# Moving two gate/up tiles out of the attention's filler, and the sums of the input ahead of its units

## The chip, the cores and the metric

The kernel runs on one core of a Trainium2 chip. The metric is the device time of one execution in microseconds. The core has TensorE (PE: matmuls, and weight loads as PEld), VectorE (DVE), ScalarE (ACT), GpSimd (POOL) and SyncE (SP, which here issues DMAs). Each works through its own instructions in order; they wait for each other by semaphores.

## The reference

Input x is 2048 × 640, 32 heads of 20, a window of 256 and a gated feed-forward of 1728.

```python
xn = _layernorm(x)
q, k, v = split_heads(xn @ wqkv)                     # wqkv 640 x 1920
scores = jnp.einsum("bhqd,bhkd->bhqk", q, k) * (Dh ** -0.5)
mask = (idx[:, None] - idx[None, :] >= 0) & (idx[:, None] - idx[None, :] < 256)
p = softmax(jnp.where(mask, scores, -1e9))
o = jnp.einsum("bhqk,bhkd->bhqd", p, v)
h = gelu(xn @ w_gate) * (xn @ w_up)                  # 640 x 1728 each
return x + o @ wo + h @ w_down
```

## The kernel before

**Arithmetic.** Activations and weights are split into a high and a low fp32r part (xh, xl; wqh, wql), and a dense product is three passes over the five blocks of 128 inputs: 15 matmuls of 128 × 512 for one tile of 128 outputs and one of the four chunks of 512 tokens.

**Stages.** First comes the layer norm chunk by chunk, with transposes into xh and xl, the first half of V (`proj_v`) and the first tiles of q and k (tile 0 and tile 5) for chunks 0 to 2. Then comes the attention: 32 units (8 groups of 4 heads × 4 chunks), each of 14 slots (NS), behind a ramp of 12 slots. Then the gate and up products of the remaining tiles, in which two chunks are joined by a scheme of seven products in place of eight (`gate_up_pair`, L953; the seven-product stage), and last the down projection (L1220).

**The attention.** A unit reads a *stack*: qs and ks, which `load_stack` (L494) loads from DRAM buffers qd and kd. `max_pair` forms scores (L523) and DVE takes their row maxima (L527); `max_end` turns these into an extra row of qs; `exp_piece` forms the scores again (L582) and ACT exponentiates them (L584) into P; `clear` has POOL zero the parts of P outside the window (L595, L598); `av_unit` multiplies with V (L609) one unit later and stores the result. Score, maximum and AV products share a ring of six PSUM banks.

**The order.** In the attention, the order on PE, ACT, DVE, POOL and SP is that in which the code emits it (`manual_schedule`). `attention()` goes from slot to slot: `at(slot, fn)` and `defer(n, fn)` put a step n slots ahead, `when_free` puts it into a list from which `release(n)` takes n steps in certain slots. Ahead of the attention a scheduler sets the order, except on PE for one chunk.

**The filler.** PE's remaining time in a slot is filled from a generator, `filler()`: projections of q and k (`proj_qk`), the second half of V (`V1_AT` says after which set) and gate/up tiles (`gate_up_fill`), in the order of the list `sets`. Each slot pulls RATE/NS matmuls, each slot of the ramp 2·RAMP. What the filler hasn't taken of the 14 gate/up tiles is left to the seven-product stage: NFA tiles and the last are in the filler.

**Saving q and k.** For each `proj_qk`, `save_qk` has ACT take the upper part (L277), DVE the remainder r (L273, one buffer), ACT the middle part (L258), POOL the lower part pt (L259), and SP store the three (L268) into qd or kd.

**The sums.** The seven-product stage reads sums of the input's two chunks that are kept in DRAM, td. `x_sums(p, k, half)` makes four of these for chunk pair p, input block k and a half chunk of 256 tokens: ten POOL instructions (L740), which POOL takes in groups of one to three for one result, and four stores (L744) on SP. Results are in tiles with two buffers. p, k and half have two values each, so there are 80 such instructions. Before, XS0 and XSN put them into units 1 to 27.

Of the kernel before, what the change touches and what calls it, by code (L numbers as in the profile page):

```python
# [9 lines left out]
F32 = mybir.dt.float32  # L10
# [20 lines left out]
NS = 14  # L31
BURSTS = 0, 4, 8
SCORES = {0: range(0, 1), 2: range(1, 5), 4: range(5, 7), 8: range(7, 9), 10: range(9, 12)}
RATE = 34.05
V1_AT = "gu", 0, 3
VEARLY = 2
VLEAD = 40
POOL_SLOTS = 13, 0, 1, 2, 3, 4, 5, 6, 7
MXD = 6
KSLOT = 9  # L40
LAG = 3, 5, 4, 4, 4, 4, 3, 3, 4, 3, 2, 1, 1, 1
NFA = 4
HD = D // 2
HR = 5
NQD = 9
OWN = 4, 5
WARM = 64
XS0, XSN = 24, 50
RAMP = 4.0
GAP = 16  # L50
VW = 1408
# [19 lines left out]
def block_kernel(ctx, tc, x, wqk, wv, wgu, wdo, wdl, out):  # L71
# [124 lines left out]
    def at(slot, fn, *a):  # L196
        acts.setdefault(slot, []).append((fn, a))
# [23 lines left out]
    def flush():  # L221
        while lates:
            fn, a = lates.pop(0)
            fn(*a)
# [4 lines left out]
    def defer(n, fn, *a):  # L229
        if now[0] is None:  # L230
            fn(*a)
        else:
            at(now[0] + n, fn, *a)

    def load_qk(t):
        raw = wrp.tile([128, KT, 128], F32, name="wr", tag="wr")
        nc.sync.dma_start(raw, wqk[t])
        return raw
# [106 lines left out]
    def first_chunk(xs, wr0, wr5, lp):  # L345
# [74 lines left out]
                save_qk(5 * i, 0, dn[i])  # L420
        return w0, w5, mv

    v0 = []
    with tc.tile_pool(name="lp", bufs=1, side="right") as lp:
        xs = [ln_load(t, lp) for t in range(2)]
        wr0 = load_qk(0)
        xs += [ln_load(t, lp) for t in range(2, 4)]
        warm = lp.tile([128, 256], BF, name="warm")[:, 0:128]
        nc.vector.memset(warm, 0.0)
        ps = psd.tile([128, C], F32, name="ps_u", tag="dn")  # L430
        for i in range(WARM):
            nc.tensor.matmul(ps[:, 0:128], warm, warm, start=True, stop=True)
        wr5 = load_qk(5)
        prep = load_v(0, v0, lp)
        next(prep)
        xs += [ln_load(t, lp) for t in range(4, 8)]
        w0, w5, mv1 = first_chunk(xs, wr0, wr5, lp)
        run(prep)
        v0 = v0[0]
        ones = lp.tile([4, 2 * C], BF, name="ones")  # L440
        nc.gpsimd.memset(ones, 0.0)
        nc.gpsimd.memset(ones[0:2], 1.0)
        for i in range(NK):
            for j in (0, 2):
                nc.sync.dma_start(ks[i][SR:64, j:j + 2].rearrange("p j t -> p (j t)"), ones)
        for c in range(1, NC):
            ln_scale(xs[4 * c:4 * c + 4], lp, mv1 if c == 1 else None)
            vs = [proj_v(v0, 4 * c - 4 + i, None if i % 2 else (psm, "mx")) for i in range(4)]
            if c == 1:
                with tc.manual_schedule(engines={mybir.EngineType.PE}):  # L450
                    lead = (cost for gen in vs for cost in gen)
                    for _ in range(VLEAD):
                        next(lead)
                    ln_turn(4 * c, xs[4 * c:4 * c + 4])
                    run(lead)
            else:
                ln_turn(4 * c, xs[4 * c:4 * c + 4])
            if c + 1 < NC:
                xs += [ln_load(t, lp) for t in range(4 * c + 4, 4 * c + 8)]
            if c == 1:  # L460
                for i in range(NQ):
                    for j in (0, 2):
                        nc.sync.dma_start(qs[i][SR + 2:64, j:j + 2].rearrange("p j t -> p (j t)"), ones[2:4])
            if c == 2:
                for z in range(4):
                    band = mask if z == 0 else lp.tile([128, D], F32, name="xi", tag="xi", bufs=8)[:, 0:288]
                    nc.gpsimd.memset(band, 0.0)
                    nc.gpsimd.affine_select(out=band, in_=band, pattern=[[1, 288]], compare_op=OP.is_ge,
                                            fill=NEG, base=32 * z - 1, channel_multiplier=-1)
                    nc.gpsimd.affine_select(out=band, in_=band, pattern=[[-1, 288]], compare_op=OP.is_ge,  # L470
                                            fill=NEG, base=256 - 32 * z, channel_multiplier=1)
                    if z:
                        nc.gpsimd.tensor_copy(mask[32 * z:32 * z + 32], band[32 * z:32 * z + 32])
                raws1 = [load_qk(1), load_qk(6)]
            if c < NC - 1:
                run(*vs)
                run(proj_qk(0, w0, c), proj_qk(5, w5, c))
            else:
                run(*[proj_v(v0, 4 * c - 4 + i) for i in range(VEARLY)])
# [204 lines left out]
                                   lambda k: xh[:, k, cs], lambda k: xl[:, k, cs], KT)  # L684
            defer(1, *((late, c4) if i else (c1,)))

    sets = [("qk", 1), ("qk", 2), ("qk", 3), ("gu", 0), ("qk", 4)]
    sets += [("gu", f) for f in range(1, NFA)] + [("gu", NF - 1)]
    pools = (wp, None), (hp, 2)
    rest = []  # L690

# [34 lines left out]
            ws = nxt  # L726
        rest.append(ws)

    def x_sums(p, k, half):
        w = C // 2  # L730
        a, b = (slice((2 * p + i) * C + half * w, (2 * p + i) * C + half * w + w) for i in (0, 1))
        eh, el = xh.bitcast(F32), xl.bitcast(F32)
        live = {}

        def tile_of(i):
            live[i] = ap.tile([128, w], F32, name="tx", tag="tx")
            return live[i]

        def pool(o, i, j, op):
            nc.gpsimd.tensor_tensor(out=o, in0=i, in1=j, op=op)  # L740

        def store(i):
            t = live[i]
            defer(4, lambda: nc.sync.dma_start(td[p][i][:, k, half * w:half * w + w], t))  # L744

        def s1():
            pool(tile_of(1), eh[:, k, b], eh[:, k, a], OP.subtract)

        def s2():
            pool(live[1], live[1], el[:, k, b], OP.add)  # L750

        def s3():
            pool(live[1], live[1], el[:, k, a], OP.subtract)
            store(1)

        def s4():
            pool(tile_of(2), eh[:, k + 2, b], live[1], OP.subtract)

        def s5():
            pool(live[2], live[2], el[:, k + 2, b], OP.add)  # L760
            store(2)

        def s6():
            pool(tile_of(4), eh[:, k + 2, a], live[2], OP.subtract)

        def s7():
            pool(live[4], live[4], el[:, k + 2, a], OP.add)
            store(4)

        def s8():  # L770
            pool(tile_of(3), eh[:, k + 2, b], eh[:, k, b], OP.subtract)

        def s9():
            pool(live[3], live[3], el[:, k + 2, b], OP.add)

        def s10():
            pool(live[3], live[3], el[:, k, b], OP.subtract)
            store(3)

        return s1, s2, s3, s4, s5, s6, s7, s8, s9, s10  # L780

    NU = NG * NC
    stream = ((u, i) for u in range(NU) for i in range(8))
    fill = filler()
# [15 lines left out]
    def pull_fill(n):  # L800
        debt[0] += n
        while debt[0] > 0:
            debt[0] -= next(fill, 1.0)

    def attention():
        now[0] = -1
        load_stack(0)
        load_stack(1)
        load_stack(2)
        for i, (p, k, half) in enumerate((p, k, half) for p in range(NC // 2) for k in range(2) for half in range(2)):  # L810
            for j, fn in enumerate(x_sums(p, k, half)):
                at(XS0 + XSN * i + 2 * j, when_free, fn)
        for i in range(12):
            now[0] = i - 13
            for fn, a in tick():
                fn(*a)
            if i % 2 == 0:
                pull_max(2, now[0])
            flush()
            pull_fill(2 * RAMP)  # L820
        pull_fill(GAP / 2)
        pull_max(2, now[0])
        pull_fill(GAP / 2)
        for u in range(NU + 1):
            for i in range(NS):
                T = now[0] = NS * u + i
                for fn, a in tick():
                    fn(*a)
                if i in BURSTS:
                    pull_max(2, T)  # L830
                if i == 0 and u:
                    av_unit(u - 1)
                    flush()
                    pull_max(2, T)
                for s in SCORES.get(i, ()) if u < NU else ():
                    exp_piece(u, s)
                flush()
                if i in POOL_SLOTS or T < NS:
                    release(2)
                if u + 3 < NU and i in (KSLOT, 12):  # L840
                    load_stack(u + 3, (int(i == KSLOT),))
                pull_fill(RATE / NS)
        while acts or idle:
            now[0] += 1
            for fn, a in tick():
                fn(*a)
            flush()
            release(2)
        assert not idle
        now[0] = None  # L850
        run(fill)
        assert not acts
# [656 lines left out]
```

## Time and profile before

| | |
|---|---|
| median of 3 runs | 1046.38 us (1045.62 to 1047.34) |
| profiled execution | 1046.71 us, span 1045.0 us |
| instructions of PE | 9533 matmul records, 99% of the span busy |
| DVE, ACT, POOL busy | 69%, 49%, 32% |
| first score matmul of the attention | at 62.42 us |
| first AV matmul (unit 0) | at 103.62 us |
| seven-product stage | from 583.30 us on, 220.37 us, 972 matmuls |

A row of a timeline has the start in us, the time it took, the engine, the line of the code, the operation, output<-inputs with their shapes, how many instructions it joins, and in brackets how long the engine stood idle ahead of it and for what. A group's row ends in busy us, mean ns | idle us ahead of it. A row of waits has the total, the number and the longest. SPq is SP's queue of DMA issues.

### The profile page before, as it was taken

To read this page: it belongs to the slowest core of one execution; us is meant where nothing else is said; L and a number is where in the kernel's file an instruction comes from. 1 tells how busy PE (TensorE), PEld (TensorE's weight loads), DVE (VectorE), ACT (ScalarE), POOL (GpSimd) and SP (SyncE) were. 2 spreads that over 40 slices of the span, in tenths; PEclk is the share of its full clock that TensorE was granted. 3 is DMA by queue.
4 is the path that set the end of the run, shared out by engine and by line. 5 is a ranking of instruction groups with operands and counts; after the bars stand their busy time and mean duration, and the time that the engine had idled before them with its cause. 6 is when DMAs were issued, how large, how long until landed. Compare 5 with 4: busy or idle time off the path is not lost.

```text
span 1045.0 us, 25814 instructions
## 1 busy us (share of the span) xinstructions
PE 1034.0 (99%) x9533; PEld 826.2 (79%) x9533; DVE 717.1 (69%) x2007; ACT 513.6 (49%) x1088; POOL 335.9 (32%) x511
## 2 busy tenths in 40 slices
PE   8999999999999999999999999999999999999998
PEld 8987666666677766666667888888888999999998
DVE  8745656666655556666663678877656888888887
ACT  4444666765665666555656522223324553333332
POOL 5222767766464458464634111110110000000000
PEclk9999999999999999999999999999999999999999
DMA  5552465545332355444322556677217864443342
GB/s 200 189 150 61 136 185 157 174 152 183 98 117 74 106 148 153 129 131 140 103 80 82 191 193 235 220 254 246 100 61 255 272 232 137 136 128 114 124 136 92
DMA packets 105192, 158.76 MB, mean 152 GB/s; under 512 B 15421, under 2 KB 60093, under 8 KB 105065
## 3 DMA queue, kind: packets, MB, share of 16 engines
q1 hardware_dynamic: 102680, 150.95, 45.1%
q10 hardware_dynamic: 2384, 6.16, 1.8%
q8 instruction: 75, 1.23, 0.5%
q14 instruction: 53, 0.43, 0.1%
HBM read 101.78 MB, written 54.92 MB: 150 GB/s over the span
## 4 chain that ended last, share of the span: by engine, by line
PE 89%; DVE 3%; DMA 3%; POOL 2%; SPq 1%; ACT 1%; issue 1%; DVEq 0%; POOLq 0%
PE ps_g L953 21%; PE ps L1220 21%; PE ps_d L110 19%; PE ps_e L582 7%; PE ps_v L110 7%; PE ps_o L609 7%; PE ps_m L523 4%; PE ps_g L110 1%; DMA qs<-qd 1%; SPq L494 1%; PE ps_t L181 1%; DMA qd<-pt 1%; POOL pt L259 1%; PE ps_d L356 1%; POOL wql L643 0%
## 5 line engine op out<-in xcount | busy, mean ns | idle before, releaser
L527 DVE CUSTOM_DVE_ANT_0 junk<-ps_m,mask 128x288 bf16<-128x288 f32 (+2 forms) x512 | 227.9, 445 | 155.0 <-PE ps_m L523 97.2
L584 ACT ACTIVATE P<-ps_e 128x512 f32<-128x512 f32 (+2 forms) x384 | 195.6, 578 | 59.8 <-PE ps_e L582 56.1
L1220 PE MATMUL ps<-wb,at 128*128 128x320 f32 x999 | 155.9, 309 | 0.0
L1220 PEld LDWEIGHTS ps<-wb,at 128*128 128x128 f32 x999 | 148.9, 188 | 0.2
L595 POOL TENSOR_SCALAR_AFFINE_SELECT P<-P 128x512 f32<-128x512 f32 x128 | 84.6, 663 | 139.1 <-ACT P L584 138.1
L582 PE MATMUL ps_e<-qs,ks 124*128 124x128 bf16 (+2 forms) x704 | 107.4, 277 | 0.6 <-DVE mx L527 0.5
L110 PE MATMUL ps_d<-xh,wqh 128*128 128x512 f32 x350 | 104.3, 410 | 0.0
L110 PE MATMUL ps_d<-xl,wqh 128*128 128x512 f32 x350 | 104.3, 409 | 0.0
L110 PE MATMUL ps_d<-xh,wql 128*128 128x512 f32 x350 | 103.9, 409 | 0.0
L1220 PE MATMUL ps<-wt,at 128*128 128x320 f32 x552 | 89.3, 309 | 0.4 <-DVE u L1058 0.4
L582 PEld LDWEIGHTS <-ks 124*128 124x128 bf16 x704 | 50.9, 98 | 46.5 <-issue 29.0
L609 PE MATMUL ps_o<-P,v 128*32 128x384 f32 (+2 forms) x1408 | 84.9, 386 | 0.7 <-POOL P L598 0.7
L1220 PEld LDWEIGHTS ps<-wt,at 128*128 128x128 f32 x552 | 82.9, 188 | 0.9 <-DVE u L1058 0.9
L598 POOL TENSOR_SCALAR_AFFINE_SELECT P<-P 128x512 f32<-128x512 f32 x112 | 70.3, 638 | 33.6 <-ACT P L584 33.6
L1174 ACT ACTIVATE at<-ss 128x512 fp32r<-128x512 f32 x59 | 37.3, 632 | 87.6 <-DVE ss L1058 87.5
L103 POOL TENSOR_TENSOR wql<-wr,wqh 128x640 fp32r<-128x640 f32 x11 | 17.6, 1607 | 174.8 <-PE ps_g L953 149.5
L609 PEld LDWEIGHTS ps_o<-P,v 128*32 128x32 f32 x1408 | 41.0, 109 | 40.5 <-issue 20.4
L110 PEld LDWEIGHTS ps_d<-xh,wql 128*128 128x128 f32 x350 | 63.9, 189 | 11.1 <-issue 0.4
L110 PEld LDWEIGHTS ps_d<-xl,wqh 128*128 128x128 f32 x350 | 63.8, 189 | 10.4 <-issue 0.2
L110 PEld LDWEIGHTS ps_d<-xh,wqh 128*128 128x128 f32 x350 | 63.5, 189 | 10.7 <-issue 0.2
L259 POOL TENSOR_TENSOR pt<-r,pt 128x512 bf16<-128x512 f32 x40 | 46.8, 1169 | 63.2 <-ACT pt L258 63.0
L613 ACT ACTIVATE ob<-ps_o 128x512 f32<-128x512 f32 x32 | 19.1, 598 | 86.3 <-PE ps_o L609 76.1
(194 smaller groups left out, 1846.8 us busy)
## 6 DMA issues: line engine op xcount, KB each, us to landing
hr<-hd SPq DMA_DIRECT2D x104, 128.0 KB
hd<-he SPq DMA_DIRECT2D x50, 256.0 KB
wr<-wgu SPq DMA_DIRECT2D x27, 320.0 KB
qs<-qd SPq DMA_DIRECT2D x64, 120.0 KB
ks<-kd SPq DMA_DIRECT2D x64, 120.0 KB
xi<-x SPq DMA_DIRECT2D x16, 320.0 KB
qs<-qd SPq DMA_DIRECT2D x64, 80.0 KB
ks<-kd SPq DMA_DIRECT2D x64, 80.0 KB
```

The lines of the kernel that those rows point to most:

```text
L110: nc.tensor.matmul(ps, a(k), b(k), start=n == 0, stop=n == 3 * nk - 1)
L259: nc.gpsimd.tensor_tensor(out=pt[:, l, :], in0=r, in1=pt[:, 1, :], op=OP.subtract)
L523: nc.tensor.matmul(ps[32 * h:32 * h + 32, lo:hi], q[rows, j, q0:q0 + 32], keys, start=True, stop=True, tile_position=(64 * r, 32 * h))
L527: nc.vector.tensor_tensor_reduce(out=junk[:, 0:n], in0=ps[:, 0:n], in1=mask[:, 288 - n:288], scale=1.0, scalar=NEG, op0=OP.add, op1=OP.max ...
L582: nc.tensor.matmul(ps[:, col:col + n], k[0:QROWS, j, kc:kc + 128], q[0:QROWS, j, q0:q0 + n], start=True, stop=True)
L584: nc.scalar.activation(pt[:, j, lo:hi], ps[:, lo:hi], AF.Exp, scale=SCALE)
L595: nc.gpsimd.affine_select(out=a, in_=a, pattern=[[0, 4], [1, 128]], compare_op=OP.is_ge, fill=0.0, base=0, channel_multiplier=-1)
L598: nc.gpsimd.affine_select(out=a, in_=a, pattern=[[0, 4], [-1, 128]], compare_op=OP.is_ge, fill=0.0, base=-1, channel_multiplier=1)
L609: nc.tensor.matmul(o[32 * j:32 * j + 32, q0:q0 + n], v[:, w0_:w0_ + 32], pt[:, j, col:col + n], start=i == 0, stop=i == len(todo) - 1, ski ...
L953: nc.tensor.matmul(ps, i, j, start=first and n == 0, stop=n == len(work) - 1, skip_group_check=True)
L1174: nc.scalar.activation(hi[:, 3:7], s, AF.Copy)
L1220: nc.tensor.matmul(ps[bank][:, 0:HD], *work[bank][j], start=bank not in begun, stop=final[p, bank] == n and j == len(work[bank]) - 1, skip ...
```

## The change

Two gate/up tiles go from the filler to the seven-product stage (NFA 4 to 2), the filler runs the four pairs of q/k tiles first and then two gate/up tiles and the last, the second half of V follows the third pair's last chunk, and a unit pulls 26.6 matmuls of filler instead of 34.05. The sums of the first chunk pair (p = 0) are made in the layer norm's stage when chunks 2 and 3 are normalized, ahead of these chunks' projections in the code, into a tile named he; those of the second pair (p = 1) start in the ramp, ten of them every six slots, two to a slot. `release(2)` now runs in each slot of the ramp. A store follows its sum by one slot instead of four (at once in the layer norm's stage).

```diff
-RATE = 34.05
-V1_AT = "gu", 0, 3
+RATE = 26.6
+V1_AT = "qk", 3, 3
-NFA = 4
+NFA = 2
-XS0, XSN = 24, 50
+XS0, XSN = -10, 6
 def x_sums(p, k, half):            # now defined ahead of the layer norm's stage
-            live[i] = ap.tile([128, w], F32, name="tx", tag="tx")
+            live[i] = (ap.tile([128, w], F32, name="tx", tag="tx") if p else
+                       hp.tile([128, C], F32, name="he", tag="he", bufs=2)[:, 0:w])
...
-            defer(4, lambda: nc.sync.dma_start(td[p][i][:, k, half * w:half * w + w], t))
+            defer(1, lambda: nc.sync.dma_start(td[p][i][:, k, half * w:half * w + w], t))
...
                 raws1 = [load_qk(1), load_qk(6)]
+            if c > 1:
+                for half in range(2):
+                    for fn in x_sums(0, c - 2, half):
+                        fn()
             if c < NC - 1:
...
-    sets = [("qk", 1), ("qk", 2), ("qk", 3), ("gu", 0), ("qk", 4)]
-    sets += [("gu", f) for f in range(1, NFA)] + [("gu", NF - 1)]
+    sets = [("qk", i) for i in range(1, 5)] + [("gu", f) for f in range(NFA)] + [("gu", NF - 1)]
...
-        for i, (p, k, half) in enumerate((p, k, half) for p in range(NC // 2) for k in range(2) for half in range(2)):
-            for j, fn in enumerate(x_sums(p, k, half)):
-                at(XS0 + XSN * i + 2 * j, when_free, fn)
+        for i, (k, half) in enumerate((k, half) for k in range(2) for half in range(2)):
+            for j, fn in enumerate(x_sums(1, k, half)):
+                at(XS0 + XSN * i + j // 2, when_free, fn)
         for i in range(12):
...
             flush()
+            release(2)
             pull_fill(2 * RAMP)
```

In the changed code the sum is line L435, its store L439, `load_stack` L552, the clears L653 and L656.

First, SP's queue at the start of the attention, before: behind the twelve loads of the first stack (qs_166, ks_169) stands the first load of the second one (qs_167), and then the stores of chunk 2's q tile.

```order
L494 DMA qs_166<-qd_84 60x1024
L494 DMA ks_169<-kd_88 40x1024
L494 DMA ks_169<-kd_88 20x1024
L494 DMA ks_169<-kd_88 60x1024
L494 DMA ks_169<-kd_88 40x1024
L494 DMA ks_169<-kd_88 20x1024
L494 DMA ks_169<-kd_88 60x1024
L494 DMA qs_167<-qd_85 40x1024
L268 DMA qd_86<-pt 80x3x512
L268 DMA qd_86<-pt 48x3x512
```

The same place after the change; td_100 to td_103 are the four results of `x_sums` for p = 0, he the tile a sum is in.

```order
L552 DMA ks_169<-kd_88 60x1024
L439 DMA td_103<-he 128x256
L268 DMA qd_86<-pt 80x3x512
L439 DMA td_102<-he 128x256
L268 DMA qd_86<-pt 48x3x512
L439 DMA td_100<-he 128x256
L268 DMA kd_90<-pt 80x3x512
L268 DMA kd_90<-pt 48x3x512
L439 DMA td_101<-he 128x256
L439 DMA td_103<-he 128x256
L552 DMA ks_169<-kd_88 40x1024
L552 DMA ks_169<-kd_88 20x1024
```

The second half of ks_169 now stands behind stores of three groups of sums and behind the stores of chunk 2's q and k.

Second, POOL from the last masks to the clears of unit 0 (P), before: between them stand six pt steps of saving q and k and two splits of weights (wql).

```order
L473 COPY mask<-xi 32x288
L259 TENSOR_TENSOR pt<-r,pt 128x512 x3
L103 TENSOR_TENSOR wql<-wr,wqh 128x640 x2
L259 TENSOR_TENSOR pt<-r,pt 128x512 x3
L595 AFFINE_SELECT P<-P 128x4x128
L598 AFFINE_SELECT P<-P 128x4x128
L595 AFFINE_SELECT P<-P 128x4x128
L259 TENSOR_TENSOR pt<-r,pt 128x512
```

After the change, the end of that stretch, with the clears of unit 0 (xh_78, xh_79 and the xl are chunks 2 and 3 of the input, tx the sums).

```order
L653 AFFINE_SELECT P<-P 128x4x128
L435 TENSOR_TENSOR tx<-tx,xl_82 128x256
L435 TENSOR_TENSOR tx<-xh_79,tx 128x256
L435 TENSOR_TENSOR tx<-tx,xl_83 128x256
L435 TENSOR_TENSOR tx<-xh_78,tx 128x256
L653 AFFINE_SELECT P<-P 128x4x128
L656 AFFINE_SELECT P<-P 128x4x128
L653 AFFINE_SELECT P<-P 128x4x128
L435 TENSOR_TENSOR tx<-tx,xl_82 128x256
```

Between the masks and the last clear that AV of unit 0 needs, POOL now has 71 sums beside what it had.

More of the change, by code (lines that the diff above doesn't have):

```diff
@@ L421, in first_chunk, with x_sums, tile_of, pool @@
         return w0, w5, mv
+    def x_sums(p, k, half):
+        w = C // 2
+        a, b = (slice((2 * p + i) * C + half * w, (2 * p + i) * C + half * w + w) for i in (0, 1))
+        eh, el = xh.bitcast(F32), xl.bitcast(F32)
+        live = {}
+        def tile_of(i):
+            live[i] = (ap.tile([128, w], F32, name="tx", tag="tx") if p else
+                       hp.tile([128, C], F32, name="he", tag="he", bufs=2)[:, 0:w])
+            return live[i]
+        def pool(o, i, j, op):
+            nc.gpsimd.tensor_tensor(out=o, in0=i, in1=j, op=op)
+        def store(i):
+            t = live[i]
+            defer(1, lambda: nc.sync.dma_start(td[p][i][:, k, half * w:half * w + w], t))
+        def s1():
+            pool(tile_of(1), eh[:, k, b], eh[:, k, a], OP.subtract)
+        def s2():
+            pool(live[1], live[1], el[:, k, b], OP.add)
+        def s3():
+            pool(live[1], live[1], el[:, k, a], OP.subtract)
+            store(1)
+        def s4():
+            pool(tile_of(2), eh[:, k + 2, b], live[1], OP.subtract)
+        def s5():
+            pool(live[2], live[2], el[:, k + 2, b], OP.add)
+            store(2)
+        def s6():
+            pool(tile_of(4), eh[:, k + 2, a], live[2], OP.subtract)
+        def s7():
+            pool(live[4], live[4], el[:, k + 2, a], OP.add)
+            store(4)
+        def s8():
+            pool(tile_of(3), eh[:, k + 2, b], eh[:, k, b], OP.subtract)
+        def s9():
+            pool(live[3], live[3], el[:, k + 2, b], OP.add)
+        def s10():
+            pool(live[3], live[3], el[:, k, b], OP.subtract)
+            store(3)
+        return s1, s2, s3, s4, s5, s6, s7, s8, s9, s10
     v0 = []
@@ L727, in filler @@
         rest.append(ws)
[L729 to L735, printed above, removed]
-            live[i] = ap.tile([128, w], F32, name="tx", tag="tx")
[L737 to L743, printed above, removed]
-            defer(4, lambda: nc.sync.dma_start(td[p][i][:, k, half * w:half * w + w], t))
[L746 to L780, printed above, removed]
     NU = NG * NC
```

## The prediction

> **What bounds the kernel now.** I read four views in this order: the page's header and busy shares, the busy time by stretches, the chain that ended last, and then the timelines of the engines around the start of the attention, since most of what the change moves lands there.
>
> ```profile
> span 1045.0 us, 25814 instructions
> PE 1034.0 (99%) x9533; PEld 826.2 (79%) x9533; DVE 717.1 (69%) x2007; ACT 513.6 (49%) x1088; POOL 335.9 (32%) x511
> ```
>
> The profiled execution took 1046.71 us, 1.7 more than its span and 0.3 above the median of 1046.38; I sum against 1046.7. PE is busy for 99% of it. So the kernel gets faster only by fewer or shorter matmuls, and slower by every microsecond in which PE must wait. From run to run, 0.2% (2.1 us) is about what a measurement of this kernel can tell from no change.
>
> ```profile
> core 0: us, PE busy (x) PEld busy (x) DVE busy (x) ACT busy (x) POOL busy (x), PEclk, DMA share, GB/s
> 50.00:75.00 25.00, 25.00 (x215) 21.39 (x221) 10.46 (x33) 10.38 (x27) 7.72 (x6) 1.00 0.44 133
> 75.00:100.00 25.00, 25.00 (x283) 19.79 (x282) 14.10 (x59) 10.85 (x37) 4.09 (x5) 1.00 0.32 95
> 400.00:425.00 25.00, 25.00 (x322) 16.32 (x321) 15.56 (x62) 16.32 (x32) 16.08 (x25) 1.00 0.57 168
> 625.00:650.00 25.00, 25.00 (x112) 20.68 (x111) 20.02 (x36) 7.59 (x16) 2.99 (x2) 1.00 0.72 252
> ```
>
> Two stretches at the start of the attention (the first two rows), one in its middle and one in the seven-product stage: PE fills each, and no other engine passes 81%. Note POOL's 7.72 and 4.09 us in the first two rows: 11.8 of 50 us. This is the room that the change fills.
>
> ```profile
> 31.26 6.84 PE ps_d L110 x30
> 118.61 2.75 PE ps_o L609 x48
> 133.61 2.79 PE ps_o L609 x48
> 583.30 220.37 PE ps_g L953 x972
> ```
>
> From the chain, in order of time: 30 filler matmuls take 6.84 us, 0.228 each; 972 of the seven-product stage 220.37 us, 0.2267 each; and the AV matmuls of two units that follow each other start 15.0 us apart, which is one unit.
>
> **The change part by part.** *The tiles.* A gate/up tile in the filler is 30 matmuls for each of 4 chunks, so two are 240; in the seven-product stage a tile is 972/9 = 108, so two are 216. 240 × 0.228 = 54.7 us leave and 216 × 0.2267 = 49.0 come, all on PE's path: **−5.7 us**. In that stage DVE is at 20.02 of 25 us; more tiles lengthen the stage at the same mix, so it doesn't become the bound.
>
> *The thinner filler.* RATE falls by 7.45 matmuls a unit, 1.70 us; units become 13.3 us long. The same DVE work then takes 15.56/25 × 15.0/13.3 = 70% of a unit, ACT's 74%; neither is a bound. But filler is also what PE does while ACT and DVE free the PSUM banks, and two slots lose 2 × 1.70/14 = 0.24 us of it.
>
> ```profile
> PE ps_o L609 <- POOL P L598: 0.7, 2, 0.5
> PE ps_e L582 <- DVE mx L527: 0.5, 2, 0.3
> POOL tx L740 <- DMA td<-tx: 4.8, 3, 4.3
> ```
>
> By the list of waits PE stood 0.5 us in all for the DVE reads. If in each of 32 units one such stretch had no slack, its 0.24 us would come through: +8. If all have slack: 0. Against it, the sums leave the steady part, where POOL was at 16.08 of 25 us, and AV's waits of 0.7 us for POOL may go: −1. I take **+1** (−1 to +8), near the rows, in which PE hardly waits.
>
> *The sums, moved ahead.* This is the main term. POOL works in order. I list first what it did in the ramp before the change.
>
> ```profile
> 45.72 0.44 POOL L473 COPY mask<-xi 32x288 f32<-32x288 f32 x1
> 54.78 1.16 POOL L259 TENSOR_TENSOR pt<-r,pt 128x512 bf16<-128x512 f32 x1 [8.62 <-ACT pt L258]
> 58.16 1.17 POOL L259 TENSOR_TENSOR pt<-r,pt 128x512 bf16<-128x512 f32 x1 [2.22 <-ACT pt L258]
> 69.77 3.09 POOL L103 TENSOR_TENSOR wql<-wr,wqh 128x640 fp32r<-128x640 f32 x2
> 95.19 0.63 POOL L595 TENSOR_SCALAR_AFFINE_SELECT P<-P 128x512 f32<-128x512 f32 x1 [7.86 <-ACT P L584]
> 104.98 0.64 POOL L595 TENSOR_SCALAR_AFFINE_SELECT P<-P 128x512 f32<-128x512 f32 x1
> 103.62 1.28 PE L609 MATMUL ps_o<-P,v 128*32 128x384 f32 x16
> 105.08 1.07 PE L609 MATMUL ps_o<-P,v 128*32 128x384 f32 x16 [0.18 <-POOL P L598]
> ```
>
> The masks are done at 45.72 + 0.44 = 46.2. The clears of unit 0 (L595, L598) run from 95.19 on, the last it needs from 104.98, and the AV matmuls of unit 0 on PE begin at 103.62 and already wait 0.18 us for a clear at 105.08. The clears thus come just in time. What a sum costs:
>
> ```profile
> 120.16 0.73 POOL L740 TENSOR_TENSOR tx<-xh,xh 128x256 f32<-128x256 f32 x1
> 120.97 1.55 POOL L740 TENSOR_TENSOR tx<-tx,xl 128x256 f32<-128x256 f32 x2
> 122.48 0.46 POOL L643 TENSOR_TENSOR wql<-wr,wqh 128x128 fp32r<-128x128 f32 x1
> L740 POOL TENSOR_TENSOR tx<-tx,xl 128x256 f32<-128x256 f32 x48 | 35.6, 742 | 1.7
> ```
>
> Mean 0.742 us; where one uses the one before, the starts are 0.81 apart (120.16, 120.97) or 0.77 (the pair). I take 0.79 with the gaps.
>
> By the order of the changed program, between the masks and the clears that AV of unit 0 needs POOL now has 71 sums, the 6 pt steps of L259, 2 splits of L103 and 6 clears. 71 × 0.742 = 52.7, or × 0.79 = 56.1; 6 × 1.17 = 7.0; 3.1 for the splits; 6 × 0.6 = 3.6. Together 66.4 to 69.8 us of work without a pause, so it ends at 112.6 to 116.0. With thinner filler PE would want the clears at 105.0 − 1.7 = 103.3. Without any wait PE loses **9.3 to 12.7 us** there. (Five sums stand ahead of the masks and one pt, where POOL had 11.84 us idle; I cost them at nothing.)
>
> ```profile
> 37.62 1.16 POOL L259 TENSOR_TENSOR pt<-r,pt 128x512 bf16<-128x512 f32 x1 [11.84 <-ACT pt L258]
> 458.10 0.74 POOL L740 TENSOR_TENSOR tx<-xh 128x256 f32<-128x256 f32 x1 [4.35 <-DMA td<-tx]
> 454.81 3.22 DMA td<-tx
> 214.62 3.01 DMA qd<-pt
> ```
>
> *Waits inside the chain.* Results go through two buffers, so the sixth sum of a group of ten waits until the store of the first result, issued after the third, has landed, with only two sums (1.6 us) between; the eighth waits likewise for the second result. Before, the sums were two slots (2.1 us) apart, which left a store about that long to land, and the list of waits shows three such stalls, 4.8 us in all, the longest the one at 458.10. From issue to landing the chain has 3.22 us there, for two stores that are issued one behind the other; for one alone I estimate 2.4. With 2.4 each group waits 2 × 0.8 = 1.6 us, and 7 groups 11; some of it falls on pt steps and clears that fill the gap, so I take **7** (3 at a landing in 1.9 us; 22 at 2.8, when the first and fourth sums of the next group wait 0.4 each as well). That puts the last clear at 116 + 7 = 123, and PE 123 − 103.3 ≈ **20 us** behind.
>
> *What is behind in SP's queue.* SP issues in order, too, and a store waits there for its sum.
>
> ```profile
> 45.85 3.12 SPq L494 DMA_DIRECT2D ks<-kd  x6
> 49.02 0.33 SPq L494 DMA_DIRECT2D qs<-qd  x1
> 55.97 0.82 SPq L268 DMA_DIRECT2D qd<-pt  x2
> 56.85 0.75 SPq L494 DMA_DIRECT2D qs<-qd  x2
> 62.42 0.38 PE L523 MATMUL ps_m<-ks,qs 60*32 60x32 bf16 x28
> ```
>
> Before, the first stack (qs and ks of unit 0) was all issued by 49.0, and PE's first score matmuls ran at 62.42. (The row at 55.97 shows how SP stops: it waited for POOL's pt of 54.78.) Now the last three loads of ks stand behind the third group's third store, that is behind 22 sums and 2 pt after 46.2: 46.2 + 22 × 0.79 + 2.3 = 65.9, and with one or two tile waits 67. Landed 2.4 us later, PE's first score matmul comes at about 69.5, **7 us** late (5 to 9.5). This wait is not added: POOL is as late at AV of unit 0 whether PE stood before it or not, as long as POOL itself doesn't wait for PE. It is the first part of the 20.
>
> *The clock in such a pause.* The cold start has a row, and the granted clock is 1.00 in all four stretches above.
>
> ```profile
> L432 PE MATMUL ps_u<-warm x64: 219/314/314, 1.2 to 7.0; 128*128 128x128 bf16 x64
> ```
>
> The same matmul has 314 ns at the median and 219 at best, so PE begins slow; no row of before shows it falling back, since it never idles long. The Trainium skill, "TensorE: Matmul & The Clock Gate", Part 1 "The HAM clock gate", says that a PE idle for a window of some 3.4 us drops to half clock until about 3.4 us of work have passed; by it each of two pauses would cost an estimated 1.7 us more, the first of them hidden in POOL's lateness, and the sum would be 1063.7. No run here shows whether that holds after a pause.
>
> **The sum:** 1046.7 − 5.7 + 20 + 1 = **1062 us**.
>
> **The rivals.** *A, faster:* POOL and the stores stay hidden. For it: POOL's 7.72 and 4.09 us of 25, and that filler between could let PE go on. It decides at the last clear of unit 0: if that comes by 103.3, PE doesn't notice, and the time is 1046.7 − 5.7 + 0 to 1 = 1041 to 1042. Against it: 66 us of work in 57 (46.2 to 103.3), each price from a row, in an order that is fixed; sums would have to take 0.61 us instead of 0.742. *B, the bare chain:* nothing waits for a store, and only the work counts: +9.3 to +12.7, 1050 to 1054. For it: the list shows only three such waits. *C, stores set the pace:* landings near 3.0 us, as in the rows of 214.62 and 454.81, or stores held in SP's queue behind others that wait for a pt: 22 us instead of 7, clear at 138, 1046.7 − 5.7 + 35 + 1 = 1077. *D, the thin filler costs:* without PSUM slack the +1 is +8; with the chain as forecast 1069. *E, the clock falls back* when PE pauses: then PE would run after each pause as at its start, 5.8 us (1.2 to 7.0) at 314 instead of 219 ns, which loses 5.8 × (1 − 219/314) = 1.8 us; the first pause's part lies inside POOL's lateness, so 1064 in place of 1062. For it: a slow start has a row; against it: no row of before has a fall. (This is the rule of the skill named above, priced from the row.) *That the change doesn't do what it says* is excluded by the order: 24 matmuls fewer, and the sums ahead of the clears.
>
> **How the numbers follow.** The forecast has 0.40 (1056 to 1068 on its own), E 0.20, which the same stretch holds, B 0.14, C 0.10, D 0.06, A 0.10. The range holds the forecast, E, D, most of B and part of C: 1049 to 1074; left out are A, the strip next to it and the end of C, some 0.18. Faster by over 0.2% is A with 0.10; within 0.2% is the strip between A and B (a chain shorter than its work by the rows), 0.03 of B's 0.14; slower 0.87.
>
> **What would show it.** Right, if PE's row at the first score matmul starts at 67 to 72 with a wait for ks or its DMA; if POOL is busy over 80% from 46 to 115 and AV of unit 0 begins at 118 to 128 behind a clear of L653 or L656; if POOL rows of the sums show waits for td stores of about 1 us, twice in each ten; and if the seven-product stage has 1188 matmuls and takes 269 us. The forecast is wrong if PE stands at 99% in 50:125 (A), if the AV starts before 117 without waits of sums (B), or if PE's idle time lies in units 1 to 31 rather than ahead of them (D).

## The result, and the profile after

The changed kernel took 1077.55 us (median of 4 runs, 1075.56 to 1081.22) against 1046.72 for the kernel before: a ratio of 1.030, 95% interval 1.0269 to 1.033. That is 31 us slower, where 15 were forecast; it lies above the range's end of 1074. It is also the time of rival C (1077), but by luck: C's 22 us of waits for stores were 9.9, as the rows below show. The profiled execution took 1076.62 us.

The page's header and busy shares of the changed kernel:

```profile
span 1074.9 us, 25862 instructions
PE 1040.9 (97%) x9509; PEld 828.8 (77%) x9509; DVE 725.6 (68%) x2029; ACT 509.5 (47%) x1088; POOL 332.2 (31%) x495
```

PE has 24 matmuls fewer and yet is busy 6.9 us longer, and it is idle for 1074.9 − 1040.9 = 34.0 us instead of 11.0. Both the idle time and the slower matmuls show in the stretches of the attention's start (columns as in the prediction; the number behind POOL's count is the granted clock, then come DMA share and GB/s):

```profile
50.00:75.00 25.00, 16.21 (x112) 13.87 (x111) 5.92 (x15) 5.96 (x17) 21.84 (x30) 0.87 0.40 121
75.00:100.00 25.00, 22.34 (x209) 17.43 (x207) 10.29 (x38) 6.93 (x18) 19.10 (x24) 0.98 0.51 155
100.00:125.00 25.00, 20.28 (x227) 15.14 (x227) 12.64 (x52) 10.72 (x33) 19.45 (x27) 0.84 0.36 119
400.00:425.00 25.00, 24.65 (x363) 15.16 (x363) 15.90 (x65) 17.63 (x36) 16.27 (x28) 1.00 0.54 161
```

POOL went from 7.72 and 4.09 us to 21.84 and 19.10, and PE from 25.00 to 16.21 and 22.34. PE's timeline shows the waits:

```profile
71.66 0.52 PE L581 MATMUL ps_m<-ks,qs 60*32 60x32 bf16 x27 [7.90 <-DMA ks<-kd]
72.11 2.50 PE L110 MATMUL ps_d<-xh,wqh 128*128 128x512 f32 x5
76.02 1.31 PE L110 MATMUL ps_d<-xl,wqh 128*128 128x512 f32 x5
100.66 1.70 PE L110 MATMUL ps_v<-wvh,xh 128*128 128x320 f32 x5 [3.32 <-DVE r L273]
122.02 0.64 PE L667 MATMUL ps_o<-P,v 128*32 128x256 f32 x8 [1.57 <-POOL P L653]
127.10 1.93 PE L667 MATMUL ps_o<-P,v 128*32 128x384 f32 x16 [4.44 <-POOL P L656]
```

The first scores wait 7.90 us for the last loads of the first stack; the AV matmuls of unit 0 wait for the clears until 127.10, where before they went on at 105.08. The wait of 3.32 us between them is POOL's, too: the remainder r has one buffer, and DVE can't write the next one before POOL's late pt (98.73 to 99.88) has read the last.

```profile
99.92 0.69 DVE L273 TENSOR_TENSOR r<-ps_d,pt 128x512 f32<-128x512 f32 x1 [5.72 <-POOL pt L259]
```

What else stood between, from SP's and POOL's timelines and the list of waits:

```profile
65.38 0.80 SPq L268 DMA_DIRECT2D kd<-pt  x2
66.86 1.94 SPq L439 DMA_DIRECT2D td<-he  x2
68.86 1.11 SPq L552 DMA_DIRECT2D ks<-kd  x3
```

```profile
47.74 0.93 POOL L435 TENSOR_TENSOR he<-xh,he 128x256 f32<-128x256 f32 x1 [1.58 <-DMA td<-he]
93.35 0.74 POOL L435 TENSOR_TENSOR tx<-xh,tx 128x256 f32<-128x256 f32 x1 [2.79 <-DMA td<-tx]
112.14 0.64 POOL L653 TENSOR_SCALAR_AFFINE_SELECT P<-P 128x512 f32<-128x512 f32 x1 [3.24 <-ACT P L642]
126.41 0.64 POOL L656 TENSOR_SCALAR_AFFINE_SELECT P<-P 128x512 f32<-128x512 f32 x1
126.99 0.64 POOL L653 TENSOR_SCALAR_AFFINE_SELECT P<-P 128x512 f32<-128x512 f32 x1
```

```profile
POOL he L435 <- DMA td<-he: 5.8, 6, 2.3
POOL tx L435 <- DMA td<-tx: 4.1, 4, 2.8
```

The seven-product stage came out as worked out, 1188 matmuls in 269.45 us:

```profile
563.16 269.45 PE ps_g L958 x1188
```

### The profile page after: what moved, and what is told of

Read it like the earlier page. It is cut to its first block, busy times and chain, and to the rows that moved or that the text cites. A ratio compares the mean times of both kernels' runs of the same rounds, so it can differ in the third digit from the quotient of the medians.

```text
span 1074.9 us, 25862 instructions
## 1 busy us (share of the span) xinstructions
PE 1040.9 (97%) x9509; PEld 828.8 (77%) x9509; DVE 725.6 (68%) x2029; ACT 509.5 (47%) x1088; POOL 332.2 (31%) x495
## 4 chain that ended last, share of the span: by engine, by line
PE 81%; POOL 5%; DMA 5%; DVE 4%; ACT 2%; issue 2%; SPq 1%; ACTq 0%; DVEq 0%; POOLq 0%
PE ps_g L958 25%; PE ps L1225 19%; PE ps_d L110 13%; PE ps_e L640 7%; PE ps_o L667 7%; PE ps_v L110 4%; PE ps_m L581 4%; POOL tx L435 2%; POOL he L435 2%; DMA td<-he 2%; PE ps_g L110 1%; ACT P L642 1%; DMA hr<-hd 1%; DMA td<-tx 1%; POOL pt L259 1%
## 5 line engine op out<-in xcount | busy, mean ns | idle before, releaser
L653 POOL TENSOR_SCALAR_AFFINE_SELECT P<-P 128x512 f32<-128x512 f32 x128 | 83.2, 652 | 148.1 <-ACT P L642 147.9
L640 PE MATMUL ps_e<-qs,ks 124*128 124x128 bf16 (+2 forms) x704 | 111.0, 278 | 3.0 <-ACT ob L671 1.0
L103 POOL TENSOR_TENSOR wql<-wr,wqh 128x640 fp32r<-128x640 f32 x13 | 20.8, 1606 | 217.7 <-PE ps_g L958 172.3
L110 PE MATMUL ps_d<-xh,wqh 128*128 128x512 f32 x270 | 85.0, 423 | 0.0
L110 PE MATMUL ps_d<-xh,wql 128*128 128x512 f32 x270 | 83.8, 418 | 0.0
L110 PE MATMUL ps_d<-xl,wqh 128*128 128x512 f32 x270 | 82.6, 414 | 0.0
L656 POOL TENSOR_SCALAR_AFFINE_SELECT P<-P 128x512 f32<-128x512 f32 x112 | 70.2, 638 | 27.4 <-ACT P L642 27.4
L581 PE MATMUL ps_m<-ks,qs 60*32 60x96 bf16 (+5 forms) x3008 | 58.0, 246 | 11.8 <-DMA ks<-kd 7.9
L987 ACT ACTIVATE hr<-hr 128x512 f32<-128x512 f32 x22 | 13.9, 632 | 111.2 <-DVE hr L961 111.2
L958 PE MATMUL ps_g<-xh,wql 128*128 128x512 f32 x198 | 66.3, 389 | 0.0
L958 PE MATMUL ps_g<-xl,wqh 128*128 128x512 f32 x198 | 66.3, 389 | 0.0
L958 PE MATMUL ps_g<-xh,wqh 128*128 128x512 f32 x198 | 66.3, 389 | 0.0
```

Source lines behind the costliest of these rows:

```text
L110: nc.tensor.matmul(ps, a(k), b(k), start=n == 0, stop=n == 3 * nk - 1)
L581: nc.tensor.matmul(ps[32 * h:32 * h + 32, lo:hi], q[rows, j, q0:q0 + 32], keys, start=True, stop=True, tile_position=(64 * r, 32 * h))
L640: nc.tensor.matmul(ps[:, col:col + n], k[0:QROWS, j, kc:kc + 128], q[0:QROWS, j, q0:q0 + n], start=True, stop=True)
L653: nc.gpsimd.affine_select(out=a, in_=a, pattern=[[0, 4], [1, 128]], compare_op=OP.is_ge, fill=0.0, base=0, channel_multiplier=-1)
L656: nc.gpsimd.affine_select(out=a, in_=a, pattern=[[0, 4], [-1, 128]], compare_op=OP.is_ge, fill=0.0, base=-1, channel_multiplier=1)
L958: nc.tensor.matmul(ps, i, j, start=first and n == 0, stop=n == len(work) - 1, skip_group_check=True)
```

## The experiments

Two things are read from each trace: where AV of unit 1 starts, which is the end of the ramp, and how long it is from there to AV of unit 31. In 30 units the thinner filler should save 30 × 1.70 = 51.0 us.

**The tiles alone, and the sums alone.** The first kernel is the one before with the tiles' part (RATE, V1_AT, NFA, sets); the second is the changed one with these four put back.

```diff
-RATE = 34.05          # second kernel: the reverse, on the changed kernel
+RATE = 26.6
-V1_AT = "gu", 0, 3
+V1_AT = "qk", 3, 3
-NFA = 4
+NFA = 2
...                    # and the list sets
```

> The kernel before with the tiles' part of the change alone (RATE, V1_AT, NFA, sets); the 80 sums stay spread over units 1 to 27. Theory (the sums in the ramp are the cost): 24 fewer matmuls give -5.7 us, the thinner filler costs the +4.6 us that the two traces show between AV of unit 5 and AV of unit 31, so 1045 to 1047 us, with AV of unit 0 at about 102. Rival (thin filler and the new order of the sets cost most of the 31 us): 1060 us or more.

> The changed kernel with RATE, V1_AT, NFA and sets as before; the sums stay ahead. Theory: PE loses 26 us up to AV of unit 1 as in the changed kernel (a little less by 1.7, since unit 0 is longer) and a few more in units 1 to 5, so 1071 to 1077 us. Rival (thin filler): about 1050 us.

The tiles alone took 1060.27 us (ratio 1.0135, 1.0103 to 1.0167), the sums alone 1067.48 us (1.02, 1.0182 to 1.0218). Each half by itself is slower. My theory missed the tiles by 13 us, where the rival (1060 us or more) came true, and the sums by 3.5. AV of units 1 and 31, before, tiles alone, sums alone, changed kernel:

```profile
118.55 1.72 PE L609 MATMUL ps_o<-P,v 128*32 128x384 f32 x28
566.18 2.26 PE L609 MATMUL ps_o<-P,v 128*32 128x384 f32 x36
```

```profile
115.79 2.58 PE L609 MATMUL ps_o<-P,v 128*32 128x384 f32 x40 [0.55 <-DVE mx L527]
529.87 2.80 PE L609 MATMUL ps_o<-P,v 128*32 128x384 f32 x48
```

```profile
142.56 2.69 PE L667 MATMUL ps_o<-P,v 128*32 128x384 f32 x44
586.13 2.26 PE L667 MATMUL ps_o<-P,v 128*32 128x384 f32 x36
```

```profile
141.38 1.93 PE L667 MATMUL ps_o<-P,v 128*32 128x384 f32 x32 [0.55 <-DVE mx L585]
546.27 2.80 PE L667 MATMUL ps_o<-P,v 128*32 128x384 f32 x48
```

The ramp ends 24.0 us late with the sums (142.56 − 118.55) and not with the tiles. From there to unit 31 it takes 447.6 us before, so 396.6 are due with thin filler. The tiles alone take 414.1, **17.5** too long; the changed kernel 404.9, **8.3** too long; the sums alone 443.6, 4.0 less than before. So the sums in the units are dearer under thin filler (9.2 us) than under thick (4.0), and thin filler with the sums gone is 8.3 us dearer than before. That is more than the 5.7 us that the fewer matmuls save. Compared like with like, both without sums in the units, it is more: 443.6 − 51.0 = 392.6 would be due, and 404.9 is 12.3 too long. How the sums cost it shows in POOL's wait for the store of a sum; the first row is the tiles alone, the second the kernel before:

```profile
POOL tx L739 <- DMA td<-tx: 14.6, 7, 3.6
```

```profile
POOL tx L740 <- DMA td<-tx: 4.8, 3, 4.3
```

and, in the tiles alone, POOL held by such a store, and PE behind POOL's clears:

```profile
180.95 0.74 POOL L739 TENSOR_TENSOR tx<-xh,tx 128x256 f32<-128x256 f32 x1 [3.30 <-DMA td<-tx]
192.00 1.57 PE L609 MATMUL ps_o<-P,v 128*32 128x384 f32 x16 [1.66 <-POOL P L598]
```

Sums come two slots apart; a slot is shorter now, and the store that a tile's reuse waits for has less time.

**Sums spread evenly.** One number: five slots between the sums of a group of ten, not two, in the kernel before and in the tiles alone.

```diff
-                at(XS0 + XSN * i + 2 * j, when_free, fn)
+                at(XS0 + XSN * i + 5 * j, when_free, fn)
```

> The kernel before with the ten sums of a group five slots apart instead of two, which spreads the 80 sums evenly over units 1 to 29. In the kernel with the sums taken out of the units, units 1 to 31 lost 4.1 us less, so at most that is to be had. Theory (groups of sums crowd POOL): 1043 to 1045 us. Rival (it is the sum of POOL's work, however spread): 1046 to 1047 us.

> The tiles' part of the change alone with the sums spread evenly, five slots apart. With the sums in groups this took 1060 us, of which 8.3 us was lost in one unit (165 to 205 us) and 6.4 in another (375 to 380 us); with the sums out of the units 9.2 us less was lost there. Theory (groups of sums delay clears and stores, and the thinner filler no longer covers it): 1051 to 1054 us. Rival (the thinner filler itself): 1058 to 1061 us.

Both came as the theory had them: 1044.37 us (ratio 0.9978, 0.9968 to 0.9987), the fastest kernel of this study, 1.8 us below the one before, and 1051.65 us (1.0051, 1.0036 to 1.0066). In neither does POOL's wait for a store of a sum appear in the list of waits. For the tiles with even sums:

```profile
115.72 2.58 PE L609 MATMUL ps_o<-P,v 128*32 128x384 f32 x40 [0.55 <-DVE mx L527]
520.73 2.58 PE L609 MATMUL ps_o<-P,v 128*32 128x384 f32 x40
```

405.0 us, as in the changed kernel: 8.4 us more than the 396.6 due. The kernel before with even sums takes 445.1:

```profile
118.58 1.72 PE L609 MATMUL ps_o<-P,v 128*32 128x384 f32 x28
563.72 2.58 PE L609 MATMUL ps_o<-P,v 128*32 128x384 f32 x40
```

Of that 394.1 would be left, so with even sums on both sides the tiles' part costs 10.9 us in the units. It isn't spread evenly: 2.7 us of it lie in one unit (AV at 157.42 and 172.91), where scores wait 0.83 and 0.81 us for loads of qs. No run changes RATE without V1_AT, NFA and sets, so it is not shown how much of this is the thinner filler and how much the new order of what it does.

The comparison with the changed kernel is close, one trace each: this kernel's span is 1049.2 us, and the changed one's 1074.9 is 25.7 longer, just as its AV of unit 1 (141.38 against 115.72) is 25.7 later. All that the sums' new place costs beside even sums lies ahead of unit 1.

**One pair of sums ahead.** First only those of the second pair (in the ramp), then only those of the first (in the layer norm's stage); the other pair's sums are put into the units, as a group of ten every 50 slots.

```diff
-            if c > 1:                                   # first kernel
-                for half in range(2):
-                    for fn in x_sums(0, c - 2, half):
-                        fn()
...
-                at(XS0 + XSN * i + j // 2, when_free, fn)   # second kernel
+                at(24 + 50 * i + 2 * j, when_free, fn)
...
+                at(74 + 50 * i + 2 * j, when_free, fn)      # first kernel, p = 0
```

> The changed kernel with the sums of the first chunk pair put into units 5 to 15 instead of the layer norm's stage; those of the second pair stay in the ramp. Theory (POOL's work ahead of the clears of unit 0): 36 sums instead of 71 stand there, behind the splits of L103 at 70 us 34 of them, 34 x 0.79 + 3.1 + 4 x 1.17 + 3.6 + 4 to 6 for stores end at about 113, 8 to 10 us after PE wants them, and the first scores start at 62.4: 1053 to 1058 us. Rival (only the first pair's stores in front of the first stack matter): 1045 to 1047 us.

> The changed kernel with the sums of the second chunk pair put into units 1 to 15; those of the first pair stay in the layer norm's stage. Theory: the first scores wait for the last loads of the first stack as in the changed kernel (about 8 us, and 2 us at a slow clock after it), but POOL is done with these sums by 82 and the clears of unit 0 come in time: 1054 to 1058 us. Rival (only POOL's lateness at the clears counts, the first wait is made up): 1045 to 1048 us.

They took 1062.11 us (1.0147, 1.0121 to 1.0173) and 1065.71 us (1.0179, 1.0159 to 1.0199), 4 and 8 us above the upper ends. I still had the thin filler too cheap: up to AV of unit 31 (534.10 and 534.21) they take 407.5 and 406.6 us, 10.9 and 10.0 more than due, where I had 4.6 for the tiles. The ramp went as expected; AV of unit 1 in the one and the other:

```profile
126.56 2.69 PE L662 MATMUL ps_o<-P,v 128*32 128x384 f32 x44 [0.55 <-POOL P L648]
```

```profile
127.61 2.64 PE L667 MATMUL ps_o<-P,v 128*32 128x384 f32 x41 [0.56 <-DVE mx L585]
```

10.8 and 11.9 us later than 115.72, against 25.7 for both. In the first it is POOL's work ahead of the clears, with no wait for the stack; in the second the wait for the stack (7.92 us) and what follows. Neither rival, by which one of the two costs nothing, holds. That 10.8 and 11.9 come near to 25.7 doesn't show that the waits add up: the first pair's sums also lengthen POOL's chain ahead of the clears.

**The first stack ahead of the sums, and halves of a tile.** The first kernel calls `load_stack(0)` before the sums; by the order, its twelve loads then stand ahead of all stores of sums, and POOL takes chunk 2's pt before the sums. The second gives the first pair's results four places in the same space.

```diff
+            if c == 2:                       # first kernel; its call in attention() goes
+                load_stack(0)
             if c > 1:
...
+            elif i in (1, 4):                # second kernel, p = 0
+                live[0] = hp.tile([128, C], F32, name="he", tag="he", bufs=2)
+                live[i] = live[0][:, 0:w]
+            else:
+                live[i] = live[0][:, w:C]
```

> The changed kernel with the twelve loads of the first stack called ahead of the sums, so that no store of a sum stands before them on SP. By its order POOL also takes chunk 2's pt of q (ready at 55 us) before the sums it did from 46 on, so its chain to the clears of unit 0 starts some 9 us later with 5 sums fewer. Theory (POOL's chain sets the end of the ramp, the first wait is inside it): first scores at 62.4, but the clears of unit 0 at 129 to 132 and the time not better, 1077 to 1082 us. Rival (the first wait and the wait for the clears add up): the first 8 us and the slow clock behind them are saved, 1066 to 1069 us.

> The changed kernel with the first pair's results in the halves of one tile (the same space, four places instead of two), so that no sum of that pair waits for a store. By its order POOL makes ten of the sums ahead of the masks instead of five, and all twelve... the six ks loads of the first stack stand behind all 40 sums' stores. Theory (POOL's chain): first scores only at about 75 to 78, but the last clear of unit 0 at 115 to 119, 8 to 10 us earlier than in the changed kernel: 1066 to 1071 us. Rival (the waits add up): the later first scores cost 4 to 6 us more, 1077 us or above.

The first took 1085.57 us (1.0371, 1.0353 to 1.0389), slower still, although PE's first scores came at 62.45: the rival, by which the time of the first wait would be saved, fails. But the edit is no clean test of it, since POOL's chain starts 9 us later. PE finds its clears at 135.25:

```profile
54.81 1.16 POOL L259 TENSOR_TENSOR pt<-r,pt 128x512 bf16<-128x512 f32 x1 [8.62 <-ACT pt L258]
```

```profile
135.25 1.94 PE L669 MATMUL ps_o<-P,v 128*32 128x384 f32 x16 [4.01 <-POOL P L658]
```

It passes the theory's 132 and 1082 as well; POOL also stood 7.85 us at one store of a sum, and PE met a wait that I hadn't foreseen:

```profile
98.61 0.83 SPq L268 DMA_DIRECT2D qd<-pt  x2
104.09 0.63 PE L110 MATMUL ps_v<-wvh,xh 128*128 128x320 f32 x1 [14.32 <-DVE r L273]
```

POOL had made that pt at 86.05; its store stood in SP's queue until 98.61, behind stores of sums and loads, ACT waited for it with the next pt, DVE's r for ACT, and PE for r. The second took 1078.03 us (1.0302, 1.0287 to 1.0317), against my theory's 1066 to 1071; the rival (1077 or above) came true. POOL was done with the first pair at 73.2 and then stood still:

```profile
85.56 1.17 POOL L259 TENSOR_TENSOR pt<-r,pt 128x512 bf16<-128x512 f32 x1 [12.38 <-ACT pt L258]
```

That pt comes from a projection behind PE's first scores, which now waited till 78.02 for a stack behind the stores of all 40 sums. So POOL waits for PE, which waits for SP, which waited for POOL: whatever is saved in the sums is lost here, and the AV of unit 1 starts at 141.93, as in the changed kernel.

**The clock.** The kernel with only the first pair ahead, with PE kept at work while it waits for the first stack (the 100 matmuls' results are not used), and that kernel again without them.

```diff
+            if i == 0:
+                pw_ = bank("ps_w")
+                for _ in range(100):
+                    nc.tensor.matmul(pw_[:, 0:128], identb, identb, start=True, stop=True)
             if i % 2 == 0:
```

> The kernel with only the first pair's sums ahead (p0_ahead), with 100 matmuls of 128 x 128 of the identity, whose results nothing uses, ahead of the first score matmul, which PE otherwise spends waiting 8 us for the first stack. Theory (a pause drops the clock to half, and PE then loses about 1.9 us): the granted clock stays at 1.00 there, the five matmuls behind the first scores take 1.4 instead of 2.5 us, AV of unit 0 begins 1.5 to 2 us earlier, and the time is 1.5 to 2 us below that of p0_ahead. Rival (the matmuls are slow for another reason, or POOL or DMA sets the pace there): no difference.

> The kernel with only the first pair's sums ahead, once more, beside the one with the extra matmuls: 1064 to 1067 us as before, and under the theory of the clock 1.5 to 2 us above it.

1065.6 us (1.0184, 1.0169 to 1.0199) and 1065.57 us (1.0183, 1.0166 to 1.02): no difference in the medians. In the traces the AV of unit 0 began 2.0 us earlier (112.62 and 114.63), but the traced execution is the fastest of the first kernel's four (1063.33). And the clock wasn't kept: the 100 matmuls left a wait of 2.24 us, and behind it five matmuls again took long.

```profile
70.54 0.38 PE L581 MATMUL ps_m<-ks,qs 60*32 60x32 bf16 x27 [2.24 <-DMA ks<-kd]
70.85 2.25 PE L110 MATMUL ps_d<-xh,wqh 128*128 128x512 f32 x5
```

What the clock costs in the total stays open by this run; what it does to the matmuls is in the rows.

## Why the prediction was wrong

**The matmuls** were right: 1188 in the stage, 269.45 us against 269.3.

**The sums** were the right mechanism, at the right places, and too small: 25.7 us by the comparison above instead of 20. The first scores came at 71.66, 9.2 us late, 7.90 of it one wait (forecast 7, 5 to 9.5). The last of the six clears was done at 127.6 instead of 123: since the masks POOL had worked for 68.4 us with the gaps (forecast up to 69.8), its waits for stores were 9.9 us instead of 7, and a term was missing, 3.24 us in which POOL waited for P, because PE was behind. I had added the condition "as long as POOL itself doesn't wait for PE" and priced it at nothing. It fails a little here and by 12.38 us in the kernel with two halves. The first wait is therefore not simply inside the last one. Missing, too, was the way from POOL's pt over r to PE: 3.32 us here, and 14.32, by way of that pt's store, in the kernel with the stack first.

**The clock** fell, as the rival E had it, and oftener than its two times. Windows of the four stretches behind the falls:

```profile
68.50:75.40 6.90, 3.74 (x35) 2.92 (x36) 1.46 (x8) 0.00 (x0) 5.84 (x9) 0.51 0.36 106
99.20:106.10 6.90, 5.44 (x20) 5.44 (x21) 2.46 (x9) 1.77 (x9) 6.38 (x9) 0.51 0.77 243
123.10:130.10 7.00, 3.00 (x35) 1.27 (x36) 0.49 (x3) 0.60 (x1) 5.88 (x10) 0.51 0.26 90
191.40:194.90 3.50, 3.50 (x12) 2.31 (x10) 2.39 (x9) 2.11 (x5) 0.87 (x1) 0.51 0.41 127
```

The five matmuls at 72.11 took 2.50 us, those at 76.02 again 1.31. PE was busy for 15.7 of these 24.3 us, so at about half the clock up to 7.8 us of work were lost, an estimate; for one fall that is 1.5 to 2.7 us, against E's 1.8. How much of it is in the total, and not inside a wait for POOL, no run shows. This agrees with the Trainium skill, "TensorE: Matmul & The Clock Gate", Part 1 "The HAM clock gate" in the fall to half and its return after a few us. An idle window of its 3.4 us stands ahead of the first fall only, though; the last section has the rows.

**The thin filler** is the step that failed most. I took +1 us, with −1 to +8, from the rows in which PE hardly waits for PSUM; the term came to 8.3 in the changed kernel (17.5 with the sums left in groups). It is made of two parts that were both mis-sized: the thinner filler with its new order costs 12.3 us where at most 8 were allowed for, and the sums that leave the units give back 4.0 where I had at most 1. A list of waits shows what is late now, not how much slack is left. From AV of unit 1 to that of unit 31 PE's waits for DVE's and ACT's reads (mx, ob) rose from 1.2 us before to 4.1, and those for loads of qs from 1.5 to 2.4; one unit (AV at 183.07 and 199.81) lost 3.9 us beside the sums alone, with two waits of the second kind and a fall of the clock. About half of the 12.3 us isn't waiting at all: PE was busy for 397.8 us, where 442.3 − 51.0 = 391.3 were due, and why stays open. In size it was rival D, which I gave 0.06, on top of the forecast rather than in its place; its reason, PSUM's readers, is a part of it.

20 became 25.7 and +1 became 8.3, together 13.0 of the 14.6 us between 1062 and the profiled 1076.6; the rest, 1.6, stands in the tiles with even sums as well (0.6 before unit 1, 1.0 in the down projection). The range ended at 1074 because it took the long chain and the dear filler as alternatives; here both came. The signs that I had named couldn't tell: the first scores at 71.66, AV of unit 0 from 119.59, the 1188 matmuls and PE's idle time ahead of unit 1 all came as for a right forecast (POOL's 79% from 46 to 115 just missed its 80), but none of them sized the filler.

## What to carry to other kernels

An engine with idle time ahead of a stage isn't free to be filled when another engine is waiting, in a fixed order, for the work that stands behind. Count the work up to the first result that is needed, and add the waits that run the other way. Filler is cover, and its price is found by thinning it, not by reading present waits. Where small steps with a store each share two buffers, spreading them out beat moving them: that one number gave 0.2%.

## What the runs showed of the hardware

PE's granted clock fell after pauses shorter than I had thought, and at no fixed time into them. The four stretches at half lasted about 6.8, 6.8, 6.8 and 3.4 us, that is two or one times 3.4. The rows are the 3.41 us ahead of each fall in the changed kernel, still at full clock:

```profile
65.14:68.55 3.41, 0.00 (x0) 0.00 (x0) 0.00 (x0) 0.00 (x0) 3.06 (x5) 1.00 0.61 190
95.86:99.27 3.41, 1.48 (x11) 1.22 (x9) 0.00 (x0) 0.74 (x2) 3.25 (x5) 1.00 0.33 82
119.76:123.17 3.41, 1.32 (x16) 0.16 (x8) 1.87 (x9) 0.63 (x1) 3.25 (x6) 1.00 0.41 132
188.02:191.43 3.41, 1.81 (x39) 1.08 (x39) 0.39 (x3) 1.55 (x4) 1.81 (x3) 1.00 0.81 244
```

PE had worked for 0, 1.48, 1.32 and 1.81 us in them. The first fall came 4.8 us into the wait of 7.90 us, the second 1.9 us into the wait of 3.32 us, the third 0.5 us into that of 4.44, and the fourth 0.6 us after PE had gone on behind two short waits:

```profile
189.93 0.19 PE L581 MATMUL ps_m<-ks,qs 60*32 60x32 bf16 x1 [0.88 <-DMA qs<-qd]
190.84 0.45 PE L581 MATMUL ps_m<-ks,qs 60*32 60x32 bf16 x31 [0.72 <-DMA qs<-qd]
```

Two waits like these, 0.83 and 0.81 us at 164.24 and 165.22 in the tiles with even sums, left the clock at 1.00 from 158 to 172, and so did a single one of 0.55 us in the changed kernel from 134 to 146. So short waits can bring the fall and needn't; how much work keeps the clock these runs don't show. It came back 2.9 to 5.4 us after the work had gone on.
